# One-core attention and softplus FFN: transposes of the float16 weights queued a step later, their lower halves made in two pieces, loads, swaps and stores merged

## The chip, the cores and the metric

The kernel runs on one core of one Trainium2 chip. The metric is device time in microseconds (us): 1411.3 is the median of three runs of the kernel before (1410.25 to 1415.76). The profile comes from one more execution, taken by the hardware profiler. Engines are named as the profile names them: PE is TensorE's matrix multiply and PEld its weight load, DVE is VectorE, ACT is ScalarE, POOL is GpSimd, SP is SyncE, which issues every DMA of this kernel.

## The reference, cut to what matters

```python
# q, k, v: 8 batches x 8 heads x 576 rows x 64, float32
scores = q @ k.T / sqrt(64)
scores = where(scores >= max(scores, -1) - tau, scores, -1e9)
attn = softmax(scores)                          # with + 1e-9 under the sum
x = (attn @ v).transpose(0, 2, 1, 3).reshape(4608, 512)
h = x @ w_in                                    # 512 -> 2048
g = maximum(h, 0) + log1p(exp(-abs(h)))         # softplus
out = g @ w_out                                 # 2048 -> 512
```

`w_in` and `w_out` arrive as float64. All products are made exact enough by splitting a float32 operand in a high and a low half, each of a type that TensorE multiplies fast.

## The kernel before, in words

**Tiles.** The work on attention is cut in 32 units, one for each batch and pair of heads. A unit has 9 tiles of 128 query rows by 576 keys: tiles 0 to 3 are head 0, tiles 5 to 8 head 1, and tile 4 (`M`) holds the 64 rows that are left of each head. The program walks over 288 tiles. The FFN is cut in ten chunks of tokens and runs between the tiles: each tile has a quota of FFN matmuls, given out where the pattern string has an `f`.

**A tile.** For each tile the program goes through the letters of `PAT = "RemhlTfpSxfvwp"`. `R` is the row maximum (`negm`) of the tile two ahead, on DVE. `e` is its exponential `e_all`, on ACT. `m` is the mask of the tile one ahead, on DVE, by which `e_all` is overwritten. `h` is the high float16 half of that tile's weights, on POOL (`weights_hi`, line 547), and `l` the low half of the tile itself, on DVE (`weights_lo`). `T` is the transposition. `S` is the scores of the tile three ahead, on PE (line 464), into one of two pairs of score banks in PSUM; a pair is free again when the mask of its earlier tile is done. `x` are the extras: preparing the next unit's keys and queries, the products with the values, the row scales. `p` is a point at which operations that were put off by `defer(n, ...)` run, n points later. Two points are in a tile.

**Two sorts of units.** In the first 8 units (`s.whole`) TensorE itself transposes the float32 weights (`whole_T`: `main` into a PSUM bank of its own, the last 64 columns, `rest`, into columns of the score banks that the scores leave free). In the 24 units after them (216 tiles) the weights are split in float16 halves that stand interleaved, 64 columns high and 64 low, in a buffer `e16` (`EB` = 3 of them); `weights_T` issues a transposing DMA to `eT` (lines 561, 562 and 565), and `values` (line 574) multiplies `eT` with the split values `vt`.

**The row scales.** At the end of a unit DVE makes the reciprocals of the row sums. In tile 1 of the next unit PE transposes them into spare columns of a score bank (line 595), ACT copies them (`rt`), one DMA writes them to DRAM (`r_d`, line 601) and, a point later, four DMAs read them back, spread over 64 partitions each (`R`, lines 608 and 609). Seven points later POOL multiplies the unit's output `xp` by `R` (line 614), and four points after that a DMA stores a part of it (`x_d`, line 620). The largest magnitude of the next unit's values (`topv`) also passes through spare columns of a score bank.

**What sets the order.** From tile 72 on, DVE's and ACT's instructions keep the order in which the program is written (class `Queue`). The order on PE, POOL and SP is the framework's scheduler's. Each engine runs its own instructions in order, and what waits holds back all that stand behind it on that engine. SP issues all DMAs, eight semaphores take turns. The swaps (`swap`, lines 429 and 430) exchange the two halves of the queries between partitions, and the scores need them.

Of the kernel before, what the change touches and what calls it, by code (L numbers as in the profile page):

```python
# [37 lines left out]
VO = (6, 7, 10, 11)  # L38
# [24 lines left out]
def tile_kernel(ctx: ExitStack, tc: tile.TileContext, q, k, v, tau, w_in, w_out, out):  # L63
# [56 lines left out]
    qm = cpool.tile([P, 2, 2, P], F32R, name="qm")  # L120
# [215 lines left out]
    def load_v(s):  # L336

        if s.whole:
            s.vn = apool.tile([P, 10, D], F32, tag="vt", bufs=2, name=f"vn_{s.i}")
            load_rows(s, s.vn, v)  # L340
            for j in range(2):
                nc.sync.dma_start(
                    s.vn.rearrange("p (h s) d -> p h s d", h=2)[j * SR:(j + 1) * SR, :, NC, :],
                    v[s.b, 2 * s.hp:2 * s.hp + 2, SM:S, :].rearrange("h p d -> p h d"),
                )
            return
        s.vn = apool.tile([P, 2, 9, D], F32, tag="vn", bufs=1, name=f"vn_{s.i}")
        for i in range(2):
            for j in range(2):
                src = v[s.b, 2 * s.hp + j]  # L350
                nc.sync.dma_start(
                    s.vn[i * SR:(i + 1) * SR, j, 1:9, :].rearrange("p (n c) d -> p n (c d)", n=2),
                    src[0:SM, :].rearrange("(n p c) d -> p n (c d)", n=2, c=NC))
            nc.sync.dma_start(s.vn[i * SR:(i + 1) * SR, :, 0, :],
                              v[s.b, 2 * s.hp:2 * s.hp + 2, SM:S, :].rearrange("h p d -> p h d"))

    def top_v(s):
# [702 lines left out]
```

## Time and profile before

| what | value |
|---|---|
| three runs, median (lowest to highest) | 1411.3 us (1410.25 to 1415.76) |
| profiled execution, its own time | 1418.82 us |
| its span, first to last instruction | 1417.1 us |
| mean granted TensorE clock | 0.973 |
| PE busy | 1296.0 us, 91% |
| DVE, ACT, POOL busy | 919.3, 920.1, 943.4 us |
| bytes moved by the DMA queue of the kernel | 157.78 MB, 50.4% of 16 engines |

The profiled execution is 7.5 us longer than the median of the runs, and 1.7 us longer than its own span. PE is busy nine tenths of the span, so what can be read is where the last tenth goes, and whether PE's clock is granted in full: a stretch's PEclk is the mean granted clock as a share of 2.4 GHz, and 0.5 is the lower of two levels, 1.2 GHz. Three stretches are told apart: up to about 360 us the units transpose on TensorE; from there to 1270 us on DMA; the last part is FFN alone.

### The profile page before, as it was taken

To read this page: it belongs to the slowest core of one execution; us is meant where nothing else is said; L and a number is where in the kernel's file an instruction comes from. 1 tells how busy PE (TensorE), PEld (TensorE's weight loads), DVE (VectorE), ACT (ScalarE), POOL (GpSimd) and SP (SyncE) were. 2 spreads that over 40 slices of the span, in tenths; PEclk is the share of its full clock that TensorE was granted. 3 is DMA by queue.
4 is the path that set the end of the run, shared out by engine and by line. 5 is a ranking of instruction groups with operands and counts; after the bars stand their busy time and mean duration, and the time that the engine had idled before them with its cause. 6 is when DMAs were issued, how large, how long until landed. Compare 5 with 4: busy or idle time off the path is not lost.

```text
span 1417.1 us, 22079 instructions
## 1 busy us (share of the span) xinstructions
PE 1296.0 (91%) x7192; PEld 772.2 (54%) x7192; DVE 919.3 (65%) x1695; ACT 920.1 (65%) x1759; POOL 943.4 (67%) x1033
## 2 busy tenths in 40 slices
PE   6988899899898989899889989898999999999998
PEld 4555555455555555555555555555555765554455
DVE  5878765546777767767777777768667776751011
ACT  5867787766576758665776657666876677753222
POOL 2576876737677778668666777778767778646242
PEclk9998999999999999999999999999999999999999
DMA  5534432213766665656656676766565655631010
GB/s 138 158 108 135 123 99 84 67 38 86 152 127 132 132 146 127 133 129 144 133 131 130 122 153 128 136 123 152 118 133 129 144 115 104 112 77 40 0 38 15
DMA packets 351107, 159.19 MB, mean 112 GB/s; under 512 B 294128, under 2 KB 330256, under 8 KB 350992
## 3 DMA queue, kind: packets, MB, share of 16 engines
q1 hardware_dynamic: 350992, 157.78, 50.4%
q8 instruction: 57, 0.93, 0.3%
q14 instruction: 58, 0.48, 0.1%
HBM read 62.92 MB, written 10.63 MB: 52 GB/s over the span
## 4 chain that ended last, share of the span: by engine, by line
PE 41%; POOL 16%; DVE 13%; ACT 12%; DMA 7%; issue 7%; SPq 4%; POOLq 0%; ACTq 0%; DVEq 0%
PE o L759 12%; PE h L695 12%; PE s L464 6%; PE pv L574 4%; ACT st L152 3%; DVE e L152 3%; PE pv L533 3%; ACT L152 3%; DVE e_all L152 3%; DVE negm L152 3%; DMA R<-r_d 2%; ACT e_all L152 2%; POOL g L176 2%; POOL e L547 2%; POOL q L132 2%
## 5 line engine op out<-in xcount | busy, mean ns | idle before, releaser
L759 PE MATMUL o<-w_o,g 128*128 128x512 f16 x1728 | 422.8, 388 | 14.0 <-POOL g L175 9.6
L695 PE MATMUL h<-xh,w_i 128*128 128x512 f16 (+1 forms) x1280 | 364.4, 361 | 1.8 <-DVE xp L152 1.3
L152 ACT ACTIVATE e_all<-s,negm 128x576 f32<-128x576 f32 x288 | 213.1, 740 | 160.5 <-DVE negm L152 154.0
L152 DVE TENSOR_REDUCE negm<-s 128x1 f32<-128x576 f32 x288 | 215.5, 748 | 135.5 <-PE s L464 102.6
L547 POOL TENSOR_SCALAR e<-e_all 128x576 f16<-128x576 f32 x216 | 202.0, 938 | 149.1 <-DVE e_all L152 140.4
L464 PE MATMUL s<-kT,qT 128*128 128x288 f32 x1024 | 226.5, 342 | 69.8 <-DVE e_all L152 38.9
L152 DVE SCALAR_TENSOR_TENSOR e_all<-s,thr,e_all 128x576 f32<-128x576 f32 x288 | 233.1, 809 | 74.7 <-ACT thr L152 27.3
L695 PEld LDWEIGHTS <-w_i 128*128 128x128 f16 x1920 | 180.3, 99 | 164.6 <-issue 11.3
L759 PEld LDWEIGHTS <-g 128*128 128x128 f16 x1728 | 161.1, 100 | 193.6 <-POOL g L175 16.3
L152 DVE SCALAR_TENSOR_TENSOR e<-e_all,e 128x576 f16<-128x576 f32 x216 | 217.0, 1005 | 36.7 <-POOL e L547 36.6
L695 PE MATMUL h<-xl,w_i 128*128 128x512 f16 (+1 forms) x640 | 231.5, 362 | 2.4 <-POOL xl L176 2.4
L464 PEld LDWEIGHTS s<-kT,qT 128*128 128x128 f32 x1024 | 162.0, 197 | 116.8 <-DVE e_all L152 62.1
L152 DVE SCALAR_TENSOR_TENSOR acc<-o,c,acc 128x512 f32<-128x512 f32 x108 | 80.3, 744 | 181.9 <-PE o L759 121.0
L176 POOL TENSOR_TENSOR g<-st,g 128x512 f16<-128x512 f32 x144 | 168.9, 1177 | 7.5
L175 POOL TENSOR_SCALAR g<-st 128x512 f16<-128x512 f32 x144 | 92.1, 644 | 106.6 <-ACT st L152 106.0
L152 ACT ACT_TABLE_LOAD x119 | 152.7, 1283 | 14.6 <-PE h L695 6.7
L152 ACT ACTIVATE st<-h,c 128x512 f32<-128x512 f32 x144 | 91.1, 683 | 69.2 <-PE h L695 68.4
L574 PE MATMUL pv<-eT,vt 128*128 128x288 f16 x864 | 131.9, 292 | 0.2
L152 ACT COPY xp<-pv 64x288 f32<-64x288 f32 (+3 forms) x136 | 50.8, 378 | 112.1 <-PE pv L574 102.0
L533 PE MATMUL pv<-gw,vn 128*64 128x256 f32 (+3 forms) x320 | 101.2, 437 | 0.0
L614 POOL TENSOR_TENSOR xp<-xp,R 128x576 f32<-128x576 f32 x32 | 46.8, 1463 | 80.8 <-DMA R<-r_d 65.6
L574 PEld LDWEIGHTS <-vt 128*128 128x128 f16 x864 | 79.9, 100 | 34.9 <-issue 2.2
(104 smaller groups left out, 1658.5 us busy)
## 6 DMA issues: line engine op xcount, KB each, us to landing
qT<-qT SPq DMA_DIRECT2D x124, 128.0 KB
vn<-in_v_dram SPq DMA_DIRECT2D x96, 128.0 KB
kn<-in_k_dram SPq DMA_DIRECT2D x32, 256.0 KB
qn<-in_q_dram SPq DMA_DIRECT2D x32, 256.0 KB
wc_i<-in_moe_w_in_dram SPq DMA_DIRECT2D x16, 512.0 KB
R<-r_d SPq DMA_DIRECT2D x64, 128.0 KB
wc_o<-in_moe_w_out_dram SPq DMA_DIRECT2D x16, 512.0 KB
out_dram<-acc SPq DMA_DIRECT2D x32, 256.0 KB
```

The source lines that it names most:

```text
L132: eng.tensor_tensor(out=out_, in0=in_, in1=hi.bitcast(F32), op=ALU.subtract)
L152: i = getattr(self.eng, name)(*args, **kwargs)
L175: nc.gpsimd.tensor_scalar(out=hi, in0=x, scalar1=1.0, scalar2=1.0, op0=ALU.mult, op1=ALU.mult)
L176: nc.gpsimd.tensor_tensor(out=lo, in0=x, in1=hi, op=ALU.subtract)
L464: nc.tensor.matmul(sp[:, hf, 0:HS], lhs, s.kT[j][:, hf * HS:(hf + 1) * HS], start=(m == 0), stop=(m == len(parts) - 1))
L533: nc.tensor.matmul(o[0:D, 0:n], s.vn[k_, 5 * j + c, :], h[k_, c, 0:n], start=(c == 0), stop=(c == NC))
L547: nc.gpsimd.tensor_scalar(out=h[:, :, 0, :], in0=s.e[t].rearrange("p (c n) -> p c n", n=SR), scalar1=2.0 ** 15, scalar2=1.0, op0=ALU.mult, ...
L574: nc.tensor.matmul(o[:, 0:HS], s.vt[:, j, slot, :], s.eT[j][:, c, x0:x0 + HS], start=(c == 0), stop=(c == 8))
L614: nc.gpsimd.tensor_tensor(out=s.xp, in0=s.xp, in1=s.R, op=ALU.mult)
L695: nc.tensor.matmul(bank[:, i * u.T:(i + 1) * u.T], wi[g, cc][:, a, e], x[cc], start=(cc == 0 and m == 0), stop=(cc == NCC - 1 and m == 2))
L759: nc.tensor.matmul(o, u.g[fc][m // 2][:, sl], wo[fc][:, m % 2, :], start=(n == 0), stop=(n == 3 * QF - 1))
```

## The change

- `weights_T` of a tile is called at step `T` of the tile behind it, and the four products with the values one tile later (`VO`). `e16` has five buffers (`HB`).
- The columns of the scores stand with the 512 main keys first. The high half is written as 576 columns in one piece, and the low half by two DVE instructions, of 512 and of 64 columns.
- The values of a float16 unit are loaded as 10 slices of 64 columns by three DMAs (before: six), their maximum is taken over 640 columns (before: 1152), and they are scaled and split once (before: twice, 576 columns each).
- `topv`, the transposed row scales and `rest` of the first 8 units get PSUM banks of the pool `ps_g`, which has four, and no longer columns of the score banks.
- The swaps of `qm` and of the first head's `qT` are merged (two DMAs, before four); the loads of the last 64 rows of keys and queries too (one, before two); `R` is read by two DMAs (before four), over all 128 partitions, from a source with the dimensions 2, 64 (of step 0) and 512 or 64; the main chunks' output rows are stored by pairs.

```diff
-VO = (6, 7, 10, 11)
+VO = (7, 8, 11, 12)
...
+HB = 5
...
-    qm = cpool.tile([P, 2, 2, P], F32R, name="qm")
+    q0 = cpool.tile([P, 2, SM + 2 * P], F32R, name="q0")
+    qm = q0[:, :, SM:].rearrange("p n (m c) -> p n m c", m=2)
...
         load_rows(s, t, src)
-        for j in range(2):
-            nc.sync.dma_start(t[j * SR:(j + 1) * SR, NC, :], src[s.b, 2 * s.hp + j, SM:S, :])
+        nc.sync.dma_start(t[:, NC, :], src[s.b, 2 * s.hp:2 * s.hp + 2, SM:S, :])
         return t
...
+        s.vn = apool.tile([P, 10, D], F32, tag="vt" if s.whole else "vn", bufs=2 if s.whole else 1, name=f"vn_{s.i}")
+        load_rows(s, s.vn, v)
         for i in range(2):
-            for j in range(2):
-                src = v[s.b, 2 * s.hp + j]
-                nc.sync.dma_start(
-                    s.vn[i * SR:(i + 1) * SR, j, 1:9, :].rearrange("p (n c) d -> p n (c d)", n=2),
-                    src[0:SM, :].rearrange("(n p c) d -> p n (c d)", n=2, c=NC))
-            nc.sync.dma_start(s.vn[i * SR:(i + 1) * SR, :, 0, :],
-                              v[s.b, 2 * s.hp:2 * s.hp + 2, SM:S, :].rearrange("h p d -> p h d"))
+            nc.sync.dma_start(
+                s.vn.rearrange("p (h s) d -> p h s d", h=2)[i * SR:(i + 1) * SR, :, NC, :],
+                v[s.b, 2 * s.hp:2 * s.hp + 2, SM:S, :].rearrange("h p d -> p h d"),
+            )
...
-            nc.tensor.matmul(spare[0], tops.to_broadcast([P, P]), ident, start=True, stop=True)
-            defer(2, take)
-
-        def take():
+            ps = ps_g.tile([P, 512], F32, tag="g", name=f"topv_{s.i}")
+            nc.tensor.matmul(ps[:, 0:P], tops.to_broadcast([P, P]), ident, start=True, stop=True)
+            defer(1, lambda: take(ps))
+
+        def take(ps):
             top = cpool.tile([P, 1], F32, tag="top", bufs=3, name=f"topv_{s.i}")
-            vec.reduce_max(top, spare[0], axis=AX.X)
+            vec.reduce_max(top, ps[:, 0:P], axis=AX.X)
...
-    def split_v(s, j):
-        if s.whole:
-            return
-        if j == 0:
-            s.vt = apool.tile([P, 2, 9, 2 * D], F16, tag="vt", bufs=2, name=f"vt_{s.i}")
-        vj = s.vn[:, j]
-        act.activation(vj, vj, AF.Copy, scale=v_scale[:, s.i:s.i + 1])
-        halves(s.vt[:, j, :, 0:D], s.vt[:, j, :, D:2 * D], vj)
+    def split_v(s):
+        s.vt = apool.tile([P, 10, 2 * D], F16, tag="vt", bufs=2, name=f"vt_{s.i}")
+        act.activation(s.vn, s.vn, AF.Copy, scale=v_scale[:, s.i:s.i + 1])
+        halves(s.vt[:, :, 0:D], s.vt[:, :, D:2 * D], s.vn)
...
             t = s.kT[j]
-            defer(1, lambda: act.copy(t[:, SR:S], ps))
+            defer(1, lambda: act.copy(t[:, 0:SM], ps))
         else:
-            t = [apool.tile([P, SM], F32R, tag=f"qT{i}", name=f"qT{i}_{s.i}_{j}") for i in range(2)]
+            if j == 0:
+                t = [q0[:, i, 0:SM] for i in range(2)]
+            else:
+                t = [apool.tile([P, SM], F32R, tag=f"qT{i}", bufs=1, name=f"qT{i}_{s.i}") for i in range(2)]
             s.qT.append(t)
-            defer(1, lambda: queries(s, t[0], t[1], ps))
-
-    def queries(s, t0, t1, ps):
+            defer(1, lambda: queries(s, j, t[0], t[1], ps))
+
+    def queries(s, j, t0, t1, ps):
...
         if s.i:
-            swap(t0, t1)
+            if j == 0:
+                swap(q0[:, 0], q0[:, 1])
+            else:
+                swap(t0, t1)
             return
...
-        act.copy(s.kT[j][:, 0:SR], ps[:, j * SR:(j + 1) * SR])
+        act.copy(s.kT[j][:, SM:S], ps[:, j * SR:(j + 1) * SR])
         if j == 0:
...
                                      AF.Copy, scale=qscale)
-            swap(qm[:, 0], qm[:, 1])
+            if s.i == 0:
+                swap(qm[:, 0], qm[:, 1])
...
     banks = [ps_s.tile([P, 2, 512], F32, tag="s", name=f"s_{i}") for i in range(SB)]
-    spare = [bank[:, 0, HS:HS + P] for bank in banks]
     nth = [0]
...
             s.sums = apool.tile([P, 9], F32, tag="sums", name=f"sums_{s.i}")
-            s.e, s.sp, s.m, s.e16, s.eT, s.bank = {}, {}, {}, {}, {}, {}
+            s.e, s.sp, s.m, s.e16, s.eT = {}, {}, {}, {}, {}
         sp = banks[nth[0] % SB]
...
         s.sp[t] = sp
-        s.bank[t] = sp
         if t == M:
...
         main = ps_g.tile([P, NC, P], F32, tag="g", name=f"tm_{s.i}_{t}")
-        rest = s.bank.pop(t)[0:SR, 1, HS:HS + P]
+        rest = ps_g.tile([P, NC, P], F32, tag="g", name=f"tr_{s.i}_{t}")[0:SR, 0, :]
         for c in range(NC):
-            nc.tensor.transpose(main[:, c, :], e[:, SR + c * P:SR + (c + 1) * P], ident)
-        nc.tensor.transpose(rest, e[:, 0:SR], ident)
+            nc.tensor.transpose(main[:, c, :], e[:, c * P:(c + 1) * P], ident)
+        nc.tensor.transpose(rest, e[:, SM:S], ident)
         s.e16[t] = main, rest
...
-        pool, tag, bufs = (apool, "e16", EB) if now["tile"] < TE or t % 2 else (wpool, "wi", WB)
-        s.e16[t] = h = pool.tile([P, 9, 2, SR], F16, tag=tag, bufs=bufs, name=f"e16_{s.i}_{t}")
-        nc.gpsimd.tensor_scalar(out=h[:, :, 0, :], in0=s.e[t].rearrange("p (c n) -> p c n", n=SR),
-                                scalar1=2.0 ** 15, scalar2=1.0, op0=ALU.mult, op1=ALU.mult)
+        pool, tag, bufs = (apool, "e16", HB) if now["tile"] < TE or t % 2 else (wpool, "wi", WB)
+        s.e16[t] = h = pool.tile([P, 2 * S], F16, tag=tag, bufs=bufs, name=f"e16_{s.i}_{t}")
+        nc.gpsimd.tensor_scalar(out=h[:, 0:S], in0=s.e[t], scalar1=2.0 ** 15, scalar2=1.0, op0=ALU.mult, op1=ALU.mult)
     def weights_lo(s, t):
-        h = s.e16[t]
-        vec.scalar_tensor_tensor(out=h[:, :, 1, :], in0=s.e.pop(t).rearrange("p (c n) -> p c n", n=SR),
-                                 scalar=2.0 ** 15, in1=h[:, :, 0, :], op0=ALU.mult, op1=ALU.subtract)
+        h, e = s.e16[t], s.e.pop(t)
+        for i, o in ((slice(0, SM), slice(S + SR, 2 * S)), (slice(SM, S), slice(S, S + SR))):
+            vec.scalar_tensor_tensor(out=h[:, o], in0=e[:, i], scalar=2.0 ** 15, in1=h[:, i],
+                                     op0=ALU.mult, op1=ALU.subtract)
...
             s.eT[j] = apool.tile([P, 9, S], F16, tag="eT", bufs=2, name=f"eT_{s.i}_{j}")
-        h = s.e16.pop(t).rearrange("p c i n -> p (c i n)")
+        h = s.e16.pop(t)
         if t == M:
-            nc.sync.dma_start_transpose(s.eT[0][:, :, SM:S], h[0:SR])
-            nc.sync.dma_start_transpose(s.eT[1][:, :, SM:S], h[SR:P])
+            for j in range(2):
+                nc.sync.dma_start_transpose(s.eT[j][:, :, SM:S], h[j * SR:(j + 1) * SR])
             return
...
     def row_scales_T(s):
-        nc.tensor.transpose(spare[1][0:9], s.rs, ident)
-        defer(1, lambda: row_scales_out(s))
-
-    def row_scales_out(s):
+        ps = ps_g.tile([P, 512], F32, tag="g", name=f"rT_{s.i}")
+        nc.tensor.transpose(ps[0:9, 0:P], s.rs, ident)
+        defer(1, lambda: row_scales_out(s, ps))
+
+    def row_scales_out(s, ps):
         rt = apool.tile([P, S], F32, tag="R", bufs=1, name=f"rt_{s.i}")[0:9, 0:P]
-        act.activation(rt, spare[1][0:9], AF.Copy, scale=1.0 if s.whole else 2.0 ** -15)
+        act.activation(rt, ps[0:9, 0:P], AF.Copy, scale=1.0 if s.whole else 2.0 ** -15)
         nc.sync.dma_start(s.r_d, rt)
...
         rows = s.r_d.rearrange("a p -> (a p)")
-        for j in range(2):
-            nc.sync.dma_start(s.R[j * D:(j + 1) * D, 0:SM], rows[j * SM:(j + 1) * SM].partition_broadcast(D))
-            nc.sync.dma_start(s.R[j * D:(j + 1) * D, SM:S],
-                              rows[2 * SM + j * SR:2 * SM + (j + 1) * SR].partition_broadcast(D))
+        for a, n in ((0, SM), (2 * SM, SR)):
+            nc.sync.dma_start(s.R[:, a and SM:(a and SM) + n],
+                              rows[a:a + 2 * n].rearrange("(j n) -> j n", j=2)[:, None, :].to_broadcast([2, D, n]))
         defer(XD - 1, lambda: scale_x(s))
...
-            dst = out[u.b * S:u.b * S + SM, :].rearrange("(p c) e -> p c e", c=NC)[:, tb, :]
-            nc.sync.dma_start(dst, a)
+            dst = out[u.b * S:u.b * S + SM, :].rearrange("(p c) e -> p c e", c=NC)
+            if u.tail:
+                nc.sync.dma_start(dst[:, tb, :], a)
+            elif tb % 2:
+                nc.sync.dma_start(dst[:, tb - 1:tb + 1, :], u.pairs[tb // 2])
...
-            times = ((s.i - 1, 0), (s.i - 1, 3), (s.i - 1, 6), (s.i - 1, 8))
-        for at_, f in zip(times, (load_v, top_v, lambda x: split_v(x, 0), lambda x: split_v(x, 1))):
+            times = ((s.i - 1, 0), (s.i - 1, 3), (s.i - 1, 7))
+        for at_, f in zip(times, (load_v, top_v, split_v)):
...
                     whole_copy(cur, t)
-                else:
-                    weights_T(cur, t)
+                if g and not tiles[g - 1][0].whole:
+                    weights_T(*tiles[g - 1])
             elif step == "h" and nxt and not nxt[0].whole:
...
     last = units[-1]
+    weights_T(*tiles[-1])
     rest = {15: lambda: row_scales_T(last), 21: lambda: values(last, 2), 24: lambda: values(last, 3)}
```

What the names in the orders below are: `e_18_4` is the high half of tile 4 of unit 18, `q_19_1` the split queries of the next unit, `g_3_6` and `g_3_7` two halves of the FFN's hidden layer, `xp` the output that is multiplied by `R`.

POOL, in unit 18, from tile 4's high half on, before:

```order
L547 TENSOR_SCALAR e_18_4_7916<-e_all 128x9x64
L614 TENSOR_TENSOR xp_7659<-xp_7659,R_7875 128x576
L547 TENSOR_SCALAR e_18_5_7978<-e_all 128x9x64
L125 TENSOR_SCALAR q_19_1_7996<-qn_7762 128x4x64
L132 TENSOR_TENSOR q_19_1_7996<-qn_7762,q_19_1_7996 128x4x64
L175 TENSOR_SCALAR g_3_6_7956<-st_6_7930 128x512
L176 TENSOR_TENSOR g_3_6_7957<-st_6_7930,g_3_6_7956 128x512
L175 TENSOR_SCALAR g_3_7_7960<-st_7_7928 128x512
L176 TENSOR_TENSOR g_3_7_7961<-st_7_7928,g_3_7_7960 128x512
```

and the same place after:

```order
L538 TENSOR_SCALAR e_18_4_7880<-e_all 128x576
L538 TENSOR_SCALAR e_18_5_7950<-e_all 128x576
L127 TENSOR_SCALAR q_19_1_7969<-qn_7738 128x4x64
L177 TENSOR_SCALAR g_3_6_7929<-st_6_7895 128x512
L134 TENSOR_TENSOR q_19_1_7969<-qn_7738,q_19_1_7969 128x4x64
L178 TENSOR_TENSOR g_3_6_7930<-st_6_7895,g_3_6_7929 128x512
L177 TENSOR_SCALAR g_3_7_7933<-st_7_7893 128x512
L606 TENSOR_TENSOR xp_7676<-xp_7676,R_7841 128x576
L178 TENSOR_TENSOR g_3_7_7934<-st_7_7893,g_3_7_7933 128x512
L538 TENSOR_SCALAR e_18_6_7988<-e_all 128x576
```

The multiply by `R` stood right behind tile 4's high half; it now stands six instructions later, behind the next tile's high half, the queries and three of the four halves of `g`.

SP, in unit 18, from the last load of `R` on, before:

```order
L609 DMA R_7875<-r_d_114 64x64
L565 DMA_TRANSPOSE eT_0_7782<-e_18_3_7864 128x9x128
L620 DMA x_d_94<-xp_7659 128x64
L561 DMA_TRANSPOSE eT_0_7782<-e_18_4_7916 128x9x64
L562 DMA_TRANSPOSE eT_1_7981<-e_18_4_7916 128x9x64
L331 DMA qn_8179<-in_q_dram 128x2x256
L429 DMA qm<-qm 64x256
L430 DMA qm<-qm 64x256
L429 DMA qT_19_0_7947<-qT_19_0_7946 64x512
L430 DMA qT_19_0_7947<-qT_19_0_7946 64x512
```

and after (`q_95` is the buffer in which `qm` and the first head's `qT` stand together):

```order
L601 DMA R_7841<-r_d_114 128x1x512
L601 DMA R_7841<-r_d_114 128x1x64
L556 DMA_TRANSPOSE eT_0_7795<-e_18_3_7830 128x9x128
L553 DMA_TRANSPOSE eT_0_7795<-e_18_4_7880 128x9x64
L553 DMA_TRANSPOSE eT_1_7992<-e_18_4_7880 128x9x64
L332 DMA qn_8152<-in_q_dram 128x2x256
L328 DMA qn_8152<-in_q_dram 128x1x64
L421 DMA q_95<-q_95 64x768
L422 DMA q_95<-q_95 64x768
L612 DMA x_d_94<-xp_7676 128x64
```

The store `x_d`, which waits for POOL's multiply, stood ahead of tile 4's transposes and of the swaps; it now stands behind both.

DVE, in unit 16, after (before, the tile's low half is one instruction, `e_16_0_6872<-e_all,e_16_0_6872 128x9x64`):

```order
L154 TENSOR_REDUCE negm_2_6892<-s_130 128x1
L154 SCALAR_TENSOR_TENSOR e_all,sums_6778<-s_131,thr_1_6843,e_all 128x576
L154 SCALAR_TENSOR_TENSOR e_16_0_6848<-e_all,e_16_0_6848 128x512
L154 SCALAR_TENSOR_TENSOR e_16_0_6848<-e_all,e_16_0_6848 128x64
L154 TENSOR_TENSOR xp_6819<-pv_1_6866,xp_6819 64x288
L154 SCALAR_TENSOR_TENSOR acc_2_6083<-o_2_2_6854,c_2_5300,acc_2_6083 128x512
L154 TENSOR_REDUCE negm_3_6927<-s_131 128x1
```

A mask, the two pieces of the low half of the tile before it, and then the next row maximum follow each other on DVE.

## Rows read from the trace of the kernel before

**Rows 1.** The page's first part: busy us, share of the span, instructions.
```profile
PE 1296.0 (91%) x7192; PEld 772.2 (54%) x7192; DVE 919.3 (65%) x1695; ACT 920.1 (65%) x1759; POOL 943.4 (67%) x1033
```

**Rows 2.** Busy time by windows; columns in the first line, clock and DMA share last.
```profile
core 0: us, PE busy (x) PEld busy (x) DVE busy (x) ACT busy (x) POOL busy (x), PEclk, DMA share, GB/s
200.00:360.00 160.00, 152.50 (x802) 86.62 (x802) 94.45 (x185) 114.41 (x237) 98.62 (x110) 0.99 0.30 76
360.00:1000.00 640.00, 575.63 (x3222) 344.31 (x3220) 471.81 (x841) 427.63 (x778) 463.13 (x501) 0.96 0.65 135
1000.00:1270.00 270.00, 262.29 (x1554) 160.34 (x1553) 186.55 (x338) 190.68 (x332) 194.10 (x210) 0.99 0.56 118
```

**Rows 3.** Waits, 360 to 1000 us: us in total, times, longest us.
```profile
POOL xp L614 <- DMA R<-r_d: 59.8, 15, 7.2
...
PE s L464 <- DVE e_all L152: 21.3, 19, 5.2
...
PE s L464 <- DMA qT<-qT: 15.8, 12, 2.2
...
PE s L464 <- DVE topv L152: 13.3, 4, 3.7
...
PE o L759 <- POOL g L175: 8.1, 7, 2.2
```

**Rows 4.** Timeline, 732.5 to 746 us: start, us, instruction [idle before <- releaser].
```profile
735.04 1.41 POOL L614 TENSOR_TENSOR xp<-xp,R 128x576 f32<-128x576 f32 x1 [6.64 <-DMA R<-r_d]
736.42 0.67 POOL L547 TENSOR_SCALAR e<-e_all 128x576 f16<-128x576 f32 x1
...
736.48 0.36 SPq L620 DMA_DIRECT2D x_d<-xp  x1
...
739.29 0.60 PE L759 MATMUL o<-w_o,g 128*128 128x512 f16 x2 [1.60 <-POOL g L175]
...
742.02 0.59 SPq L430 DMA_DIRECT2D qT<-qT  x1
...
744.46 0.50 PE L464 MATMUL s<-kT,qT 128*128 128x288 f32 x2 [1.49 <-DMA qT<-qT]
```

**Rows 5.** Two windows of 8 us, columns as in rows 2.
```profile
627.00:635.00 8.00, 7.36 (x29) 4.20 (x30) 3.60 (x6) 3.56 (x7) 6.23 (x8) 0.57 0.57 115
540.00:548.00 8.00, 7.94 (x47) 4.58 (x47) 5.67 (x10) 7.91 (x15) 4.88 (x7) 1.00 0.49 95
```

**Rows 6.** The chain that ended last, 640 to 660 us: start, us, what.
```profile
651.46 0.57 SPq L608
...
653.36 3.00 DMA R<-r_d
```

**Rows 7.** Timeline of DVE and POOL, 520 to 524 us.
```profile
521.30 0.74 DVE L152 SCALAR_TENSOR_TENSOR e<-e_all,e 128x576 f16<-128x576 f32 x1
...
521.46 1.12 POOL L547 TENSOR_SCALAR e<-e_all 128x576 f16<-128x576 f32 x1 [1.31 <-DVE e_all L152]
...
521.98 0.63 DVE L152 TENSOR_SCALAR c<-p_i,sx 128x4 f32<-128x4 f32 x1
```

**Rows 8.** Groups by line and form: busy us, mean ns of one | idle before, releasers.
```profile
L152 DVE TENSOR_REDUCE negm<-s 128x1 f32<-128x576 f32 x288 | 215.5, 748 | 135.5 <-PE s L464 102.6 <-ACT rt L152 31.5
...
L176 POOL TENSOR_TENSOR vt<-vn,vt 128x576 f16<-128x576 f32 x48 | 62.1, 1293 | 1.3
...
L547 POOL TENSOR_SCALAR e<-e_all 128x576 f16<-128x576 f32 x216 | 202.0, 938 | 149.1 <-DVE e_all L152 140.4
...
L504 PE MATMUL s<-identr,e_all 128*64 128x128 f32 x72 | 21.4, 298 | 13.2 <-ACT e_all L152 12.9
...
L152 DVE TENSOR_REDUCE topv<-s 128x1 f32<-128x128 f32 x32 | 9.0, 281 | 9.1 <-ACT e_all L152 5.1 <-ACT gw L152 3.9
```

**Rows 9.** The DMA queue: packets, MB, share of 16 engines; and the loads of R.
```profile
q1 hardware_dynamic: 350992, 157.78, 50.4%
...
R<-r_d SPq DMA_DIRECT2D x64, 128.0 KB
```

More of the change, by code (lines that the diff above doesn't have):

```diff
@@ L336, in load_v @@
     def load_v(s):
-        if s.whole:
-            s.vn = apool.tile([P, 10, D], F32, tag="vt", bufs=2, name=f"vn_{s.i}")
-            load_rows(s, s.vn, v)
-            for j in range(2):
-                nc.sync.dma_start(
-                    s.vn.rearrange("p (h s) d -> p h s d", h=2)[j * SR:(j + 1) * SR, :, NC, :],
-                    v[s.b, 2 * s.hp:2 * s.hp + 2, SM:S, :].rearrange("h p d -> p h d"),
-                )
-            return
-        s.vn = apool.tile([P, 2, 9, D], F32, tag="vn", bufs=1, name=f"vn_{s.i}")
@@ L357, in top_v @@
+        load_rows(s, s.vn, v)
+        for i in range(2):
+            nc.sync.dma_start(
+                s.vn.rearrange("p (h s) d -> p h s d", h=2)[i * SR:(i + 1) * SR, :, NC, :],
+                v[s.b, 2 * s.hp:2 * s.hp + 2, SM:S, :].rearrange("h p d -> p h d"),
+            )
     def top_v(s):
         tops = cpool.tile([P, 1], F32, tag="vtop", bufs=2, name=f"vtop_{s.i}")
-        vn = s.vn.rearrange("p s d -> p (s d)" if s.whole else "p h s d -> p (h s d)")
-        vec.tensor_reduce(tops, vn, axis=AX.X, op=ALU.max, apply_absolute_value=True)
+        vec.tensor_reduce(tops, s.vn.rearrange("p s d -> p (s d)"), axis=AX.X, op=ALU.max, apply_absolute_value=True)
@@ L372, in top_v @@
         defer(2, spread)
-    def split_v(s, j):
-        if s.whole:
-            return
-        if j == 0:
-            s.vt = apool.tile([P, 2, 9, 2 * D], F16, tag="vt", bufs=2, name=f"vt_{s.i}")
-        vj = s.vn[:, j]
-        act.activation(vj, vj, AF.Copy, scale=v_scale[:, s.i:s.i + 1])
-        halves(s.vt[:, j, :, 0:D], s.vt[:, j, :, D:2 * D], vj)
+    def split_v(s):
+        s.vt = apool.tile([P, 10, 2 * D], F16, tag="vt", bufs=2, name=f"vt_{s.i}")
+        act.activation(s.vn, s.vn, AF.Copy, scale=v_scale[:, s.i:s.i + 1])
+        halves(s.vt[:, :, 0:D], s.vt[:, :, D:2 * D], s.vn)
     def split_k(s):
@@ L571, in values @@
         o = ps_g.tile([P, 512], F32, tag="g", name=f"pv_{s.i}_{g}")
-        for c in range(9):
-            slot = 0 if c == 0 else 1 + 4 * ((c - 1) % 2) + (c - 1) // 2
-            nc.tensor.matmul(o[:, 0:HS], s.vt[:, j, slot, :], s.eT[j][:, c, x0:x0 + HS], start=(c == 0), stop=(c == 8))
+        order = (0, 5, 1, 6, 2, 7, 3, 8, 4)
+        for n, c in enumerate(order):
+            nc.tensor.matmul(o[:, 0:HS], s.vt[:, 5 * j + (c if c <= NC else c - NC - 1), :],
+                             s.eT[j][:, c, x0:x0 + HS], start=(n == 0), stop=(n == 8))
         defer(1, lambda: values_out(s, g, o))
@@ L606, in load_R @@
         rows = s.r_d.rearrange("a p -> (a p)")
-        for j in range(2):
-            nc.sync.dma_start(s.R[j * D:(j + 1) * D, 0:SM], rows[j * SM:(j + 1) * SM].partition_broadcast(D))
-            nc.sync.dma_start(s.R[j * D:(j + 1) * D, SM:S],
-                              rows[2 * SM + j * SR:2 * SM + (j + 1) * SR].partition_broadcast(D))
+        for a, n in ((0, SM), (2 * SM, SR)):
+            nc.sync.dma_start(s.R[:, a and SM:(a and SM) + n],
+                              rows[a:a + 2 * n].rearrange("(j n) -> j n", j=2)[:, None, :].to_broadcast([2, D, n]))
         defer(XD - 1, lambda: scale_x(s))
@@ L733, in parts_of @@
         if u.tail:
-            spare = [("kT", 2), ("qT0", 2), ("qT1", 2), ("nat", 2), ("e16", EB)]
+            spare = [("kT", "kT", 2), ("qT0", "qT1", 1), ("nat", "nat", 2), ("e16", "e16", HB)]
             i = later_g[0] % (NG + len(spare))
@@ L737, in parts_of @@
             if i >= NG:
-                tag, bufs = spare[i - NG]
-                pool, tags = apool, (tag, tag)
+                *tags, bufs = spare[i - NG]
+                pool = apool
         gh, gl = [pool.tile([P, TC], F16, tag=tags[i], bufs=bufs, name=f"g{i}_{u.n}_{fc}") for i in range(2)]
@@ L770, in project_out @@
             u.acc += [t[:, 0, :], t[:, 1, :]]
+            u.pairs.append(t)
         a = u.acc[tb]
@@ L879, in tile_kernel @@
         u.T = SM if main else QB * SR
-        u.h, u.l, u.acc, u.g, u.st, u.full = [], [], [], {}, {}, []
+        u.h, u.l, u.acc, u.g, u.st, u.full, u.pairs = [], [], [], {}, {}, [], []
         u.scaled, u.unscaled = set(), set()
```

1 line of the change is left out of this document (removed).

## The prediction

> **What bounds the kernel now.** I read the busy shares first. PE is at 91%, the next engine at 67% [rows 1]: of the profiled execution's 1418.8 us PE works in 1296.0, and a change to the work of DVE, ACT or POOL counts only where PE waits for it. The busy time by windows then says where PE idles. Between 200 and 360 us it is busy 152.5 of 160 (95%), between 1000 and 1270 us 262.3 of 270 (97%), but between 360 and 1000 us, where the units with float16 weights run, only 575.6 of 640 (90%), and there the granted clock is 0.96, against 0.99 on either side [rows 2]. So 64 us of idle PE lie in that stretch, and with a clock of 0.96 another 0.04 x 640 = 26 us of work at full speed are lost in it. No other engine is full there: DVE has 74%, POOL 72%, ACT 67% [rows 2]. What PE loses is order, not volume.
>
> The waits of the stretch name the places [rows 3]. POOL waits 59.8 us, 15 times, for the load of R: 4.0 us at each unit's end. PE's own waits, next to 21.3 us for DVE's mask, which frees the score banks, are 15.8 us for the swapped queries, 13.3 us for the bank in which the values' maximum (topv) stands, and 8.1 us for POOL's halves of g. The timeline of one unit ties these to R [rows 4]. POOL stands idle for 6.64 us in front of the multiply by R at 735.04; behind it come, one after the other, the next high half, the queries and the halves of g; PE waits 1.60 us for g at 739.29. SP has its x_d store behind the same multiply (736.48), and behind the store the transposes and swaps; the last swap is issued at 742.02, and PE waits 1.49 us for it at 744.46. After such a hole the clock falls: the 8 us from 627 us on have a clock of 0.57, near 1.2 GHz, and 29 matmuls, where 8 us at clock 1.00 have 47 [rows 5].
>
> **The change, part by part, against the profiled 1418.8 us.**
>
> *R and what stands behind it.* The multiply by R moves six instructions down POOL's order. These take the time from 736.42 to about 741 in the timeline, some 4.6 us, and they are work that POOL has anyway. The mean wait for R is 59.8 / 15 = 4.0 us, so if R lands when it does now, most multiplies find it there. On SP the x_d store now stands behind the swaps, so these no longer wait for POOL. Topv leaves the score bank, so scores no longer wait for its reader on DVE. The PE waits that hang on this are 15.8 + 13.3 + 8.1 = 37.2 us. I do not take all of it. The last low half of g and the next tile's high half still stand behind the multiply, and the units differ (the longest wait for R is 7.2 us, above 4.6). I take two thirds: -25 us. The bounds are 0 and -37.
>
> *R's own load* is one DMA of 128 rows instead of two of 64, 262 kB. Its issue gets shorter by two steps of about 0.6 us, and now the load takes 3.00 us after its last issue [rows 6]. No row shows a load from a source in two repeated rows, so I bound it. The queue moved 157.78 MB with 50.4% of 16 engines over 1417.1 us, which is 13.8 GB/s for each busy engine [rows 9]. At that rate 262 kB take 1.2 us on all 16 engines and 19 us on one. I take the present form's time, since the nearest row is the same bytes from the same source; the other end is rival B.
>
> *The clock.* If two thirds of the holes behind R go, some of the half-clock stretches go with them. Of the 26 us I take a third, -9 (bounds 0 and -20): holes for DVE's mask remain, and they too can be followed by one.
>
> *The low half in two pieces.* Work on DVE grows by one instruction for each of 216 tiles. Its own price: a reduction of 576 columns takes 748 ns and one of 128 columns 281 ns [rows 8], that is 1.04 ns a column and 0.15 us for the instruction; the columns are the same in sum. But DVE and POOL do not run side by side here. The low half at 521.30 ends at 522.04; POOL's high half is on from 521.46 to 522.58, and the DVE instruction behind the low half, on 128x4 elements, takes 0.63 us and ends at 522.61, just as POOL does [rows 7]. So the second piece can wait for what POOL has begun, at most the 0.94 us that a high half takes on average [rows 8]. Between 0.15 and 0.94 I take the middle, 0.55 us, as rows 7 lie between them too: 216 x 0.55 = 119 us of DVE, of which 150 tiles, 82 us, fall in the window from 360 to 1000 us. There DVE goes from 472 to 554 of 640 (87%). PE waits for DVE's mask 19 times [rows 3]; those waits grow by 0.55 us each, 10 us, and a few that are now just met will join: +13 us (bounds: +3 at 0.15 us; +60 if half of the 119 us comes through, rival A).
>
> *The first units.* PE waits 12.9 us in front of the transposes into spare columns, for ACT's reading of the same bank [rows 8]. These go. In exchange 72 `rest` tiles, 32 topv tiles and 32 row-scale tiles take turns in the four banks that main transposes, hidden layer, projections and products share, and each holds its bank for about a point. No row shows waits for want of a bank that I could scale. I take 0, with 13 us on each side.
>
> *Values, loads, stores.* The values' split goes from 48 instructions of 1.29 us to 24 a ninth longer (640 instead of 576 columns), 62 to about 35 us, with its high halves and ACT's scaling in proportion. POOL has 177 us idle in the window and ACT 212 [rows 2], so this frees time on engines that are not the bound: 0. DMA share is 0.65 there; fewer issues shorten SP's turns but PE names no load among its waits other than the swaps, which are counted: 0. The transposes a step later cost nothing as long as the products with the values, moved a tile later too, find eT: 0, covered by that tile of 640 / 150 = 4.3 us, and if the cover failed, PE would wait for eT.
>
> Sum: -25 - 9 + 13 = -21, so 1398 for the profiled execution. This execution was 1418.8 where the median of the runs is 1411.3, a ratio of 0.9947; on the runs' scale 1390 us.
>
> **The rivals.**
>
> *A: DVE becomes the bound (slower).* The second piece waits for POOL at every tile. For it: rows 7, and 87% of DVE in the window already at my middle value; at 0.94 us for each of the window's 150 tiles it has 472 + 141 = 613 of 640, 96%. Against it: POOL has idle time, and DVE waits too, so that many second pieces find POOL at rest. Half of the 119 us on the path instead of 13 gives -25 - 9 + 60 = +26: 1445 for the profiled execution, 1437 on the runs' scale. From about 93% of DVE in the window on I would expect this.
>
> *B: R lands later, and the gain is given back.* The source's outer dimension is now 2. Were the load served by two engines, 262 kB would take 9.5 us (131 kB at 13.8 GB/s) in place of 1.2; less 1.2 for two issues, R would land 7 us later, while the multiply's turn comes 4.6 us later. POOL's wait would then be about 6.4 us instead of 4.0, with the last half of g and the next two high halves behind it. Of the PE waits only the 15.8 us for the swaps would go; the 8.1 us for g and what topv's bank stood for (13.3) would grow by 6.4 / 4.0, +13; with the low half's +13 and no gain of the clock: +10, 1421 on the runs' scale. If only part of that comes about, 1411. The Trainium skill, "DMA: Bandwidth & Descriptors", section "Why a DMA increments its semaphore by 16 and not by 1", says that the number of engines is the largest, up to 16, that divides the slowest dimension of both patterns, which would be two here. No row of this trace shows such a load; by that rule this rival would be the case.
>
> *C: more is won.* All 37 us go, the clock gives 20 back and the second piece costs 0.15 us: -37 - 20 + 3 = -54, 1358 on the runs' scale. For it: that one cause, R, stands behind three waits and the clock. Against it: waits of PE for DVE and for the clock's return remain.
>
> **How the numbers follow.** About 0.5%, 7 us, is what a measurement of this kernel can tell from no change. The forecast, between 1372 and 1404, has a chance of 0.43; C 0.11; B, between 1404 and 1424, 0.27; A, from 1418 up, 0.19. Faster by over 0.5% (below 1404) are the forecast and C, and a little of B: 0.55. Within 0.5% is the lower two thirds of B and a little of the forecast's and A's edges: 0.19. Slower: the rest of B and A, 0.26. The range from 1355 to 1432 leaves out part of C and the upper half of A.
>
> **What would show it.** In the window from 360 to 1000 us of the new trace, scaled: POOL's wait for R under 20 us (right) or above 60 (B); no wait of PE for the swapped queries and for topv; a granted clock of 0.97 or more; DVE's second pieces with a mean near 0.5 us, and PE's wait for DVE's mask about 34 us, not 80 (A). In the first 360 us no more than 13 us of waits for banks. The forecast is wrong if the R wait is gone and the time is not lower, for then the PE waits were not R's, or if DVE's share in the window passes 93%.

## The result, and the profile after

The changed kernel takes 1418.87 us (median of 20 runs, 1410.28 to 1427.38), the kernel before 1414.88 us in 20 runs beside it: a ratio of 1.0031, 95% interval [1.0017, 1.0045]. The forecast was 1390 us and faster; the kernel is slower by 0.3%, by the bound of 0.5% no change that counts. The profiled execution took 1422.03 us, with a span of 1420.1.

The page's first part of the changed kernel answers to [rows 1]: PE's busy time is up by 10 us for the same 7192 matmuls, DVE's by 76 us, POOL's down by 48.

```profile
PE 1306.4 (92%) x7192; PEld 770.4 (54%) x7192; DVE 995.2 (70%) x1911; ACT 906.3 (64%) x1735; POOL 895.8 (63%) x985
```

The time at which each unit's first row maximum on DVE (every ninth of 288) ends shows in which stretch the time went. Units are counted from 0, unit 8 is the first with float16 weights, the columns are the profiled executions, and a_R4 is an experiment below:

| first row maximum of | before | changed | a_R4 | changed against before |
|---|---|---|---|---|
| unit 4 | 139.9 | 145.0 | 131.6 | +5.1 |
| unit 8 | 318.4 | 327.8 | 308.4 | +9.4 |
| unit 9 | 360.0 | 381.8 | 355.7 | +21.8 |
| unit 20 | 786.1 | 797.2 | 749.9 | +11.1 |
| unit 31 | 1223.8 | 1226.1 | 1171.2 | +2.3 |
| end of the span | 1417.1 | 1420.1 | 1365.2 | +3.0 |

So from unit 9 to unit 31 the kernel did get faster, by 21.8 - 2.3 = 19.5 us. That this is near the -21 of the sum is luck: the clock and the wait for the swaps, below, did not do what the sum has for them. Up to unit 9 it lost 21.8 us: 9.4 us in the eight units that transpose on TensorE, where the sum had 0, and 12.4 us in unit 8. The waits of the changed kernel between 50 and 360 us point to the reason in one line (engine, line, what it waited for: us in total, times, longest):

```profile
POOL xp L606 <- DMA R<-r_d: 35.8, 5, 15.7
```

The timeline of POOL shows the longest of them, and the chain of waits what such a load takes after its issue, 9.08, 9.66 and 8.36 us, against 3.00 in [rows 6]:

```profile
317.82 1.41 POOL L606 TENSOR_TENSOR xp<-xp,R 128x576 f32<-128x576 f32 x1 [15.69 <-DMA R<-r_d]
```

```profile
89.85 9.08 DMA R<-r_d
...
127.24 9.66 DMA R<-r_d
...
356.92 8.36 DMA R<-r_d
```

These are the loads on the chain; over all 32 units the merged load of 256 KB has a median of 7.8 us from the start of its issue to its landing, and the loads of 64 rows in the kernel before have 3.0. The merged load of R is slow; this is rival B's mechanism. In the later units it hides from that line. Waits of the changed kernel, 360 to 1000 us, which answer to [rows 3]:

```profile
PE s L455 <- DMA q<-q: 24.9, 12, 3.2
...
PE s L455 <- DVE e_all L154: 10.1, 20, 0.8
...
POOL xp L606 <- DMA R<-r_d: 7.1, 4, 6.4
PE o L751 <- POOL g L177: 7.0, 2, 6.2
```

POOL's wait for R fell from 59.8 to 7.1 us and topv is gone from PE's waits, as forecast. But PE's wait for the swapped queries rose, from 15.8 to 24.9 us, though the swaps no longer stand behind POOL's multiply. The timeline of SP and PE in one unit shows how:

```profile
776.78 1.12 SPq L601 DMA_DIRECT2D R<-r_d  x2
778.04 6.65 SPq L556 DMA_TRANSPOSE eT<-e  x1
784.79 3.58 SPq L553 DMA_TRANSPOSE eT<-e  x2
...
789.71 0.53 SPq L421 DMA_DIRECT2D q<-q  x1
...
793.97 0.82 PE L455 MATMUL s<-kT,q 128*128 128x288 f32 x2 [3.18 <-DMA q<-q]
```

The transposing DMA behind the load of R keeps SP for 6.65 us, so the swap is issued 12.9 us after the load, and PE stands for 3.18 us. Then its clock falls, as behind the holes of [rows 5]: three windows of 8 us have 0.96, 0.61 and 1.00.

```profile
core 0: us, PE busy (x) PEld busy (x) DVE busy (x) ACT busy (x) POOL busy (x), PEclk, DMA share, GB/s
786.00:794.00 8.00, 4.79 (x27) 2.54 (x24) 5.32 (x9) 7.43 (x12) 6.72 (x7) 0.96 0.71 150
794.00:802.00 8.00, 8.00 (x32) 4.58 (x33) 3.76 (x7) 2.73 (x5) 5.54 (x6) 0.61 0.69 126
802.00:810.00 8.00, 7.96 (x45) 4.32 (x43) 7.96 (x17) 2.46 (x6) 4.18 (x4) 1.00 0.45 114
```

In the whole stretch the clock is 0.96, no better than in [rows 2], and the DMA share rose with fewer bytes a second:

```profile
360.00:1000.00 640.00, 586.42 (x3254) 344.55 (x3255) 532.02 (x1003) 425.13 (x772) 441.43 (x478) 0.96 0.74 130
```

### The profile page after: what moved, and what is told of

The parts are those of the page before. It is cut to its first block, busy times and chain, and to the rows that moved or that the text cites. A ratio compares the mean times of both kernels' runs of the same rounds, so it can differ in the third digit from the quotient of the medians.

```text
span 1420.1 us, 21687 instructions
## 1 busy us (share of the span) xinstructions
PE 1306.4 (92%) x7192; PEld 770.4 (54%) x7192; DVE 995.2 (70%) x1911; ACT 906.3 (64%) x1735; POOL 895.8 (63%) x985
## 4 chain that ended last, share of the span: by engine, by line
PE 39%; DVE 20%; ACT 16%; DMA 9%; issue 7%; POOL 7%; SPq 2%; DVEq 0%; POOLq 0%; ACTq 0%
PE o L751 13%; PE h L687 10%; PE s L455 6%; DVE e L154 6%; ACT L154 5%; DVE e_all L154 5%; ACT st L154 4%; DMA q<-q 4%; DVE negm L154 4%; PE pv L524 4%; PE pv L565 3%; DMA R<-r_d 2%; ACT e_all L154 2%; DVE acc L154 1%; POOL g L178 1%
## 5 line engine op out<-in xcount | busy, mean ns | idle before, releaser
L538 POOL TENSOR_SCALAR e<-e_all 128x576 f16<-128x576 f32 x216 | 210.0, 973 | 226.0 <-DVE e_all L154 225.7
L154 DVE SCALAR_TENSOR_TENSOR e<-e_all,e 128x512 f16<-128x512 f32 (+1 forms) x432 | 312.5, 763 | 2.7 <-POOL e L538 2.5
L455 PE MATMUL s<-kT,q 128*128 128x288 f32 x768 | 159.3, 333 | 58.5 <-DMA q<-q 30.4
L178 POOL TENSOR_TENSOR g<-st,g 128x512 f16<-128x512 f32 x144 | 174.8, 1216 | 6.3
L455 PEld LDWEIGHTS s<-kT,q 128*128 128x128 f32 x768 | 116.7, 196 | 103.0 <-DVE e_all L154 57.9
L565 PE MATMUL pv<-eT,vt 128*128 128x288 f16 x864 | 126.4, 291 | 3.8 <-DVE xp L154 3.5
L455 PE MATMUL s<-kT,qT 128*128 128x288 f32 x512 | 107.9, 333 | 8.9 <-DVE e_all L154 8.1
L524 PE MATMUL pv<-gw,vn 128*64 128x256 f32 (+3 forms) x320 | 105.9, 452 | 2.5 <-ACT gw L154 2.5
```

What stands on the lines that cost most here:

```text
L154: i = getattr(self.eng, name)(*args, **kwargs)
L178: nc.gpsimd.tensor_tensor(out=lo, in0=x, in1=hi, op=ALU.subtract)
L455: nc.tensor.matmul(sp[:, hf, 0:HS], lhs, s.kT[j][:, hf * HS:(hf + 1) * HS], start=(m == 0), stop=(m == len(parts) - 1))
L524: nc.tensor.matmul(o[0:D, 0:n], s.vn[k_, 5 * j + c, :], h[k_, c, 0:n], start=(c == 0), stop=(c == NC))
L538: nc.gpsimd.tensor_scalar(out=h[:, 0:S], in0=s.e[t], scalar1=2.0 ** 15, scalar2=1.0, op0=ALU.mult, op1=ALU.mult)
L565: nc.tensor.matmul(o[:, 0:HS], s.vt[:, 5 * j + (c if c <= NC else c - NC - 1), :], s.eT[j][:, c, x0:x0 + HS], start=(n == 0), stop=(n == 8))
```

## The experiments

Twelve kernels ran, each timed beside the kernel before on the same chip. The ratio given is to that kernel. All compute the full reference.

**R's load and the PSUM banks.** `a_R4` is the changed kernel with the four loads of R:

```diff
-        for a, n in ((0, SM), (2 * SM, SR)):
-            nc.sync.dma_start(s.R[:, a and SM:(a and SM) + n], ...)     # two DMAs, 128 rows
+        for j in range(2):
+            nc.sync.dma_start(s.R[j * D:(j + 1) * D, 0:SM], rows[...].partition_broadcast(D))
+            nc.sync.dma_start(s.R[j * D:(j + 1) * D, SM:S], rows[...].partition_broadcast(D))
```

> The changed kernel (1418.9 us), with R loaded by four DMAs of 64 rows again, as before; all else as changed. Theory 1 (the merged load of R is slow: in the changed kernel it lands 7.9 us after its issue instead of 3.0, POOL waits 43.9 us for it in the first 382 us, and SP stands for it before the next transpose): POOL's wait for R falls under 10 us in the first 382 us, the ninth unit begins at least 10 us earlier than at 381.8 us, PE's 24.9 us of waits for the merged swap between 360 and 1000 us halve, and the time is 1393 to 1405. Theory 2 (the first units lose by the PSUM banks that now carry more): the ninth unit begins at 378 us or later and the time is 1412 to 1420.

Measured: 1367.93 us, ratio 0.9684 [0.9664, 0.9704]. That is 51 us below the changed kernel and 25 us below theory 1's range: the form of R's loads had taken back a gain of 3%. Windows and waits, 360 to 1000 us:

```profile
360.00:1000.00 640.00, 604.82 (x3478) 360.43 (x3478) 569.33 (x1052) 453.19 (x822) 461.93 (x498) 1.00 0.65 135
```

```profile
PE s L455 <- DVE e_all L154: 20.7, 32, 1.0
...
PE s L455 <- DMA q<-q: 0.6, 3, 0.2
```

The wait for the swaps is gone and the clock is granted in full. The same unit on SP, with two DMAs more for R:

```profile
735.55 0.60 SPq L602 DMA_DIRECT2D R<-r_d  x1
736.25 1.33 SPq L556 DMA_TRANSPOSE eT<-e  x1
739.26 2.61 SPq L553 DMA_TRANSPOSE eT<-e  x2
...
743.25 0.51 SPq L421 DMA_DIRECT2D q<-q  x1
```

This holds for the other units too. Over some 23 units between 360 and 1270 us the transpose behind the last load of R keeps SP for 1.31 us in the median here and for 6.25 us in the changed kernel; the first swap is issued 9.5 us after the first load of R here and 11.7 us in the changed kernel. From the issue of the second swap to its landing it is 3.4 us in both, so the swaps are late because they are issued late.

`a_spare` puts `rest`, topv and the transposed row scales back into the score banks:

```diff
-        rest = ps_g.tile([P, NC, P], F32, tag="g", name=f"tr_{s.i}_{t}")[0:SR, 0, :]
+        rest = s.bank.pop(t)[0:SR, 1, HS:HS + P]     # topv in spare[0], rT in spare[1] likewise
```

> The changed kernel with the last 64 transposed columns of the first units, the values' maximum and the row scales back in the spare columns of the score banks. Theory 1: the ninth unit still begins at about 380 us, and the time stays within 1414 to 1424. Theory 2 (banks): the ninth unit begins at 360 to 370 us and the time is 1398 to 1410.

Measured: 1421.95 us, 1.0065 [1.0047, 1.0082]; unit 9 begins at 386.1 us. Theory 2 falls. With both edits (`a_R4_spare`):

> Both of the other two edits. Theory 1: as with R alone, 1393 to 1405. Theory 2: as with the banks alone. If both matter, 1380 to 1393.

Measured: 1383.06 us, 0.9787 [0.9767, 0.9807]. The number lies in the range for "both matter", but by luck: the second edit does not add to the first, it takes 15 us back. With R early the new banks are worth these 15 us, 10.7 at unit 8 and 5.2 at unit 9. Why they give only 3 us while R is late (`a_spare` against the changed kernel) was not followed up.

The other way round, `b_R2` puts the merged load into the kernel before (the diff above, reversed).

> The kernel before (1411 to 1415 us) with R loaded by two DMAs of 128 rows, as changed. There the multiply by R stands right behind tile 4's high half on POOL and already waits 4.0 us a unit for R. Theory 1: R lands some 5 us later, POOL waits 8 to 9 us in each of 32 units, and the time rises by 15 to 60 us, to 1428 to 1470. Theory 2, or R's engines do not matter: within 7 us of 1413.

Measured: 1526.05 us, 1.0806 [1.0783, 1.0828], dearer than expected. There the multiply stands early on POOL, and the halves of g are behind it:

```profile
POOL xp L613 <- DMA R<-r_d: 116.0, 14, 10.8
...
PE o L758 <- POOL g L175: 49.7, 14, 8.8
...
PE o L758 <- POOL g L176: 30.2, 10, 7.6
```

**Which way the load costs.** `a_R4_dead` leaves R's four loads and adds a load that nobody waits for; `a_R4_dead16` is its control. Both have three float16 buffers (`HB = 3`) instead of five; without the added load that is `a_R4_HB3` below, 1369.40 us.

```diff
+    dead = cpool.tile([P, SM], F32, name="dead")
# a_R4_dead, behind the four loads of R:
+        nc.sync.dma_start(dead, rows[0:2 * SM].rearrange("(j n) -> j n", j=2)[:, None, :].to_broadcast([2, D, SM]))
# a_R4_dead16, at the same place:
+        nc.sync.dma_start(dead, rows[0:SM].partition_broadcast(P))
```

> The changed kernel with R in four loads and three float16 buffers (1369.4 us), and behind them one more load of 256 KB, in the merged form with the two-row source, into a tile that nothing reads. R lands early here, but SP's next transpose stands behind a load on two engines, and SP's issue goes up by one DMA a unit. Theory 3 (the merged load costs by what it holds up on SP and on its two engines, the swaps above all): PE's waits for the merged swap are 15 us or more between 360 and 1000 us, the clock falls to about 0.97 and the time is 1390 to 1420. Theory 4 (it costs by POOL's multiply waiting for R): 1369 to 1378.

> The control to the added load: the same bytes into the same tile that nothing reads, at the same place on SP, but from a source of one row repeated 128 times, so that its outer dimension is 128. If the number of DMA engines is what counts (theory 3), this costs only its issue: 1368 to 1376, the transpose behind it takes SP about 1.5 us. If any further 256 KB at that place cost the same: about 1407.

Measured: 1407.15 us, 0.9973 [0.9953, 0.9994], and 1368.69 us, 0.9681 [0.9660, 0.9702]. A load of the same size to the same tile costs 38 us or nothing; the two differ in the source alone, two rows of 64 repeats or one row of 128. Waits of the first, 360 to 1000 us:

```profile
PE s L456 <- DMA q<-q: 32.0, 13, 4.8
...
POOL xp L609 <- DMA R<-r_d: 1.2, 1, 1.2
```

R is there in time and PE waits for the swaps all the same. SP behind the added load, in the first and then in the control:

```profile
729.60 0.56 SPq L605 DMA_DIRECT2D dead<-r_d  x1
730.27 3.30 SPq L557 DMA_TRANSPOSE eT<-e  x1
733.67 3.87 SPq L554 DMA_TRANSPOSE eT<-e  x2
```

```profile
738.50 0.59 SPq L605 DMA_DIRECT2D dead<-r_d  x1
739.21 1.55 SPq L557 DMA_TRANSPOSE eT<-e  x1
741.59 2.83 SPq L554 DMA_TRANSPOSE eT<-e  x2
```

The medians over some 23 units between 360 and 1270 us are 3.37 us for the first of these transposes and 1.48 us in the control; the first swap is issued 11.8 us after the first load of R, 9.5 us in the control.

**The prediction's main term alone.** `b_VO` is the kernel before with `VO = (7, 8, 11, 12)`.

> The kernel before with one line changed: the four products with the values one tile later (7, 8, 11, 12). With it alone the multiply by R stands behind the next tile's high half, the queries and three halves of g on POOL, and the x_d store behind the swaps on SP, as in the changed kernel. It tests the prediction's main terms by themselves (-25 for the waits behind R, -9 for the clock). The prediction: 1372 to 1390, POOL's wait for R under 20 us between 360 and 1000 us, the clock 0.98 or more there. Rival (the transposes' own later place on SP is what counts): 1400 to 1415.

Measured: 1387.34 us, 0.9823 [0.9792, 0.9853]. One line, -24 us, in the expected range, near its slow end. The stretch has more PE and a better clock, and R is no longer among POOL's waits:

```profile
360.00:1000.00 640.00, 596.72 (x3371) 355.81 (x3369) 489.07 (x873) 450.56 (x818) 488.12 (x524) 0.98 0.68 140
```

`a_R4_Tnow` undoes the step in `a_R4` (`VO` as before, `weights_T(cur, t)` at its own tile):

> The changed kernel with R in four loads (1367.9 us), and the transposes and products with the values at their old steps again. The prediction's term for the later transposes is 0: 1361 to 1375. Rival: a transpose issued at its own tile's step waits on SP for its low half, and the swaps and R behind it come later: PE's waits for the swaps are 10 us or more between 360 and 1000 us and the time is 1378 to 1400.

Measured: 1413.02 us, 0.9987 [0.9971, 1.0003]: 45 us lost, more than the rival gave. POOL's multiply is back behind tile 4's high half, and the three waits with it:

```profile
PE s L455 <- DVE e_all L154: 33.0, 35, 2.4
PE s L455 <- DMA q<-q: 24.8, 16, 2.7
POOL xp L607 <- DMA R<-r_d: 24.5, 8, 4.4
```

**The other terms.** `a_R4_HB3` has `HB = 3`; `a_R4_kq` has the small loads of keys and queries in two again, as before the change.

> The changed kernel with R in four loads (1367.9 us) and three buffers of float16 weights instead of five, transposes a step late. If the five buffers carry the late transposes: POOL's high half or DVE waits for the buffer that a transpose three tiles back still reads, and the time is 1380 to 1410. If three are enough: 1362 to 1374.

> The changed kernel with R in four loads (1367.9 us) and the last 64 rows of keys and queries in two loads of 64 rows each again. These merged loads have the same two-row source as R's, but 32 KB only, land in 3.2 us instead of 2.2, and are not waited for on PE. Theory: within 5 us of 1368. Rival: any load on few engines costs, by what SP issues behind it: 1350 to 1362.

Measured: 1369.40 us, 0.9682 [0.9665, 0.9699], so three buffers are enough; and 1374.56 us, 0.9714 [0.9697, 0.9731], 6.6 us above `a_R4` and 5.2 above `a_R4_HB3`, which was timed on the same chip. So two loads of 16 KB, once for keys and once for queries in a unit, are some 5 to 7 us dearer than a merged one of 32 KB, a difference near the bound of 0.5%. That is 1.6 us outside the theory's range and against the rival: the two-row form costs here only where the load is large.

`b_lo2` splits the low half in the kernel before:

```diff
-        vec.scalar_tensor_tensor(out=h[:, :, 1, :], ...)
+        for c in (slice(1, 9), slice(0, 1)):
+            vec.scalar_tensor_tensor(out=h[:, c, 1, :], in0=e[:, c, :], ..., in1=h[:, c, 0, :], ...)
```

> The kernel before with nothing changed but the low half, made by two DVE instructions (eight blocks of 64 columns, then one). This sizes one term of the prediction by itself. The prediction's term: the second piece waits 0.55 us for POOL at each tile and 13 us come through: 1422 to 1430, DVE's busy time up by about 100 us. Rival (the extra time on DVE is hidden): 1408 to 1417 with the same rise of DVE's busy time. Rival A (half comes through): above 1440.

Measured: 1435.50 us, 1.0157 [1.0133, 1.0180], 21.6 us, between the prediction's term and rival A. Its two pieces (groups by form, us and mean ns) and PE's wait for the mask, 360 to 1000 us:

```profile
L152 DVE SCALAR_TENSOR_TENSOR e<-e_all,e 128x512 f16<-128x512 f32 x216 | 197.5, 915 | 16.8 <-POOL e L547 16.7
L152 DVE SCALAR_TENSOR_TENSOR e<-e_all,e 128x64 f16<-128x64 f32 x216 | 155.0, 718 | 0.0
```

```profile
PE s L464 <- DVE e_all L152: 45.3, 44, 5.6
```

`a_R4_lo1` goes the other way in `a_R4` with three buffers: the interleaved layout of before, one instruction for the low half, and the six loads and two splits of values which that layout needs.

> The changed kernel with R in four loads and three buffers (1369.4 us), and the interleaved float16 halves of before, so that the low half is one DVE instruction, with six loads of values and two splits a unit, as that layout needs. If the second piece costs here what it did on the kernel before (21.6 us), less what the merged values give back: 1350 to 1365. If DVE's time is hidden here: 1367 to 1380.

Measured: 1369.92 us, 0.9698 [0.9670, 0.9726], against 1369.40: together the split and the merged values cost nothing there. What each does by itself there is not shown.

## Why the prediction was wrong

**The step that failed is "R's own load".** It said: "I take the present form's time, since the nearest row is the same bytes from the same source". The merged load lands after 7.8 us in the median, and after 8 to 10 us on the chain, where the old one took 3.00; the term that stood at no loss measured 51 us. The bounds held the truth (1.2 to 19 us of transfer), and rival B named it; I put B at 0.27 and B was the case. What argued for B was known: the source's outer dimension had become 2. The Trainium skill ("DMA: Bandwidth & Descriptors", "Why a DMA increments its semaphore by 16 and not by 1") has a rule by which that makes two engines. The runs agree: 128 repeats of one row cost nothing, two rows of 64 repeats cost 38 us, and in the traces the semaphore of the merged load is raised three times in every one of the 32 units, once about 1.0 us after the issue began and twice at some 7.8 us, where that of each 64-row load of `a_R4` is raised 16 times. I treated a rule of the Trainium skill as one more rival, where a row for its size could not exist in the trace of before.

**B had the load right and its way to PE wrong.** It expected POOL to wait 6.4 us a unit. In the first units that is near: POOL waited 35.8 us in five times, 7.2 us each. From 360 us on POOL waited 7.1 us in all, and PE's wait for the swaps, which B let go, grew. So B's 1421 us, close to the 1418.87 measured, is luck. Of the 26.1 us by which the changed kernel is behind `a_R4` at unit 9 (381.8 - 355.7), `a_R4_dead`, with R early, has only 8.9 (364.6 - 355.7); the other 17 us are put down to POOL's wait for R by this difference. From there to the end the changed kernel lost another 54.9 - 26.1 = 28.8 us, and `a_R4_dead` 41.4 - 8.9 = 32.5 with R in time: in the later units the load costs through SP. The transposes behind it stay on SP for 6.65 us instead of 1.33, and the swaps behind those come late. Why a transpose is held there is not shown; that the two-row form of the load does it is, by the control.

**"R and what stands behind it" and "the clock" were right in their mechanism.** They made -34 together; the line that moves the multiply, alone, gave -24.4 with a clock of 0.98, and in `a_R4` the clock is 1.00. The prediction's sign of being wrong, that R's wait is gone and the time is not lower, came true, but not the reason it gives: by `b_VO` and `a_R4_Tnow` PE's waits were tied to the multiply's place, and in the changed kernel the wait for the swaps has a new cause. The late transposes, which I cost at 0 by themselves, were not tried without the later products.

**"The low half in two pieces"** was sized well on DVE: 170.4 + 159.2 in the changed kernel for 217.0 before, 113 us, against 119. In `b_lo2`, with 136 us more on DVE, 21.6 came through, where I had 13: PE's waits for the mask went from 19 to 44, and not only grew longer. In `a_R4`, together with the merged values, nothing of it is left. In the changed kernel PE waits 10.1 us for the mask from 360 us on and DVE is busy 83% (532 of 640): rival A did not occur.

**"The first units: 0"** had 13 us on each side, and at unit 8, where these units end, that held: the changed kernel is 9.4 us behind the kernel before, `a_R4` 10.0 us ahead. But the 0 hid two effects: up to there R's load costs 19.4 us (327.8 - 308.4), and with R early the new banks give 10.7. "Values, loads, stores: 0" missed some 6 us for the small loads.

The terms that were measured one at a time, -24.4 (products later, in the kernel before), -15.1 (banks), -6.6 (small loads) and about 0 (low half with values, all three in `a_R4`), add up to -46; `a_R4` is 44.3 us below the kernel before (1412.26 beside it). This is no proof that nothing is missing, for a term's size depends on the kernel it is measured in: taken out of `a_R4`, the later products with the later transposes are worth 45 us, and the low half cost 21.6 us in the kernel before. The merged swaps and the stores by pairs were not tried alone. That R's load costs 51 us does not hang on this sum, as `a_R4` differs from the changed kernel in it alone.

The range, 1355 to 1432, held the time; the direction was wrong. `a_R4` is the version to keep: 3.2% below the kernel before, 3.6% below the changed one.

## What to carry to other kernels

A merged DMA is not a cheaper DMA: look at the outermost dimension of its source. Here merging turned 64 into 2, and 256 KB took 7.8 us instead of 3.0, while the transposes queued behind it on SP were held too; 32 KB in the same form did no harm. When a trace cannot hold the price of a new operation, and a rule for it speaks against the change, the new form is to be priced by the rule first and the old form's row is the hopeful end. When a change that removes measured waits comes out at zero, look for one edit in it that gives them back, and undo edits one at a time: here several gains and one large loss stood in one diff.

## What was not expected of the hardware

- A DVE instruction on 64 columns, right behind one on 512, takes nearly as long as that one while POOL is at work: in the changed kernel 737 ns against 789 ns in the mean of 216. In 210 of the 216 tiles POOL has an instruction beside both pieces, and the second takes 752 ns in the mean; in the other 6 POOL is at rest, and it takes 217 ns.

```profile
L154 DVE SCALAR_TENSOR_TENSOR e<-e_all,e 128x512 f16<-128x512 f32 x216 | 170.4, 789 | 2.7 <-POOL e L538 2.5
...
L154 DVE SCALAR_TENSOR_TENSOR e<-e_all,e 128x64 f16<-128x64 f32 x216 | 159.2, 737 | 0.0
```

- A load of 256 KB that nobody waits for cost 38 us over 32 units, though the 16 DMA engines were not full: their busy share in the window was 0.80, 0.69 in the control, and 0.65 without either load.
